# From tile 8 on, the attention products' feature blocks rotate over the four column places and are turned back by transfers

## The chip, the cores and the metric

One core of one Trainium2 chip. The metric is device time in microseconds (us) of one launch; 847.02 us is the median of three runs of the kernel before (846.87, 847.02, 848.01). PE is TensorE, PEld its weight loads, DVE VectorE, ACT ScalarE, POOL GpSimd, SP SyncE, whose queue issues nearly all transfers (DMAs).

## What is computed

Three stages one after the other: a linear recurrence over time with decay (the attention), a feed-forward layer with a maximum of three projections, and a gated layer with a norm.

```python
for t in range(S):                       # attention, B=4, H=8, S=768, D=48
    cur = u * k[t] outer v[t]
    y[:, :, t] = r[t] @ (state + cur)
    state = w * state + k[t] outer v[t]
x = y as 3072 tokens x 384 features      # H * D = 384
h = maximum(maximum(x @ w1, x @ w2), x @ w3)          # 384 -> 768
x = h @ w_out                                         # 768 -> 384
xn = x / sqrt(mean(x*x) + 1e-6) * rms_g
out = (silu(xn @ w_gate) * (xn @ w_val)) @ w_out2     # 384 -> 1536 -> 384
```

## The kernel before

Attention goes in 24 tiles of 128 time steps of one batch row: tile i belongs to chunk c = i // 4 (six chunks) and row b = i % 4. A stage u (0 to 5) is the first layer on the 512 tokens of chunk u: 18 slots `a_l1` (six blocks f times three projections w, nine matmuls of 512 columns each) and six slots `a_out`. The tiles of chunk u + 1 and later are woven between the slots of stage u: tiles 8 to 11 in stage 1, and so on, up to tiles 20 to 23 in stage 4; stage 5 has none. After each slot the loop of the schedule runs the steps that are due, so the order on every engine is the order in which this Python code calls them. A step list gives three steps for each tile: `block(i)`, `ahead(i + 2)` and `ahead_b(i + 2)`. After each step one queued load of a later tile is issued on SP. `tick` (weight conversion) runs after some slots and puts a load, three ACT steps, one or five DVE steps and stores into the queues.

`block(i)` is: score products of the next tile (`pe_a`, tile `pa`) and their masking on DVE (`mix`, L302, into `Dg`), the outputs of tile i (`pe_y`, L352, PSUM tile `py`), their split (`fin`), and the key-value product (`pe_st`, L321, PSUM tile `pkv`), which ACT masks (L308, tile `kv`) and POOL adds to the state `T` (L327, L329). `py` has 128 partitions by 3 x 128 columns. The 384 features are 12 blocks of 32; four column places (lanes) n of PE, 32 columns each, write the partitions 32n to 32n + 31 of the three k. Place n below 3 holds offset 32n of head pair k, place 3 holds head pair 3. A block at offset 0 or 64 lies in one head and needs one product `Dg`, one at offset 32 lies in two heads and needs two; from chunk 1 on each needs one more with the state. So the places have 6, 9, 6 and 7 products, 28 in all. They are issued round by round, one product of each place that still has any. Each product of f32 numbers is two matmul instructions (passes) in the profile.

`fin` splits `py` into a high and a low part: ACT copies it to `xt[u][:, 0]` (L365), DVE writes the difference to `xt[u][:, 1]` (L366). `xt[u]` is the moving operand of the first layer (L73 to L75, PSUM tile `pl`). A `pl` bank (four in all) is freed by ACT (L412, w = 0) or DVE (L415, w = 1, 2). Four slots later PE takes it again.

Of the kernel before, what the change touches and what calls it, by code (L numbers as in the profile page):

```python
# [10 lines left out]
F32R = mybir.dt.float32r  # L11
# [5 lines left out]
ALU = mybir.AluOpType  # L17
# [14 lines left out]
HF = 2  # L32
U0T = (1, 1, 1, 1, 0, 1, 1, 1, 0, 1, 1, 1, 1, 1, 1, 0, 1, 1, 1, 0, 1, 1, 1, 1, 1, 1, 1, 1, 1, 1)
LEAD = 4
DM, FF1, FF2 = 384, 768, 1536
NB = S // 128
NT = B * NB
# [4 lines left out]
def r32(ap):  # L42
    return ap.bitcast(F32)
# [3 lines left out]
def rwkv_moe_kernel(ctx, tc, rkT, rkv, wd, ub, cst, rg, w1p, wo1p, w2p, out):  # L47
    nc = tc.nc
    act, dve, pool, pe, sync = nc.scalar, nc.vector, nc.gpsimd, nc.tensor, nc.sync
# [8 lines left out]
    tp = sT.enter_context(tc.tile_pool(name="att", bufs=1, side="right"))  # L58
# [127 lines left out]
    def load_next(n=1):  # L186
        for _ in range(n):
            if loads:
                loads.pop(0)()

    def load_tile(i):
        if i >= NT:
            return
        a = tp.tile([128, 2, NP, 128], F32, tag="raw", bufs=3, name=f"raw{i}")
        t = tp.tile([128, VO + NP * 144], F32, tag="tm", bufs=3, name=f"tm{i}")
        raw_t[i], tm_t[i] = a, t
        loads.append(lambda: sync.dma_start(a[0:64], rows64[96 * i:96 * i + 64]))
        if i < NT - 1:
            loads.append(lambda: sync.dma_start(a[64:128], rows64[96 * i + 48:96 * i + 112]))
        else:  # L200
            loads.append(lambda: (sync.dma_start(a[64:112], rows64[96 * i + 48:96 * i + 96]),
                                  sync.dma_start(a[112:128], rows64[96 * i:96 * i + 16])))
        loads.append(lambda: sync.dma_start(t[:, 0:VO], rkv[i, :, 0:VO]))
        loads.append(lambda: sync.dma_start(t[:, VO:], rkv[i, :, VO:]))
# [47 lines left out]
    def prep_raw(i):  # L252
        raw = raw_t.pop(i)
        st[i] = dict(raw=raw, tm=tm_t.pop(i))
        if i == 0:
            dve.tensor_tensor(out=raw[:, 1], in0=raw[:, 1], in1=qk[:, 1], op=ALU.mult)
            dve.tensor_tensor(out=raw[:, 0], in0=raw[:, 0], in1=qk[:, 0], op=ALU.mult)
        else:
            dve.tensor_tensor(out=raw, in0=raw, in1=qk, op=ALU.mult)

    def prep(i):
        prep_raw(i)
        s = st[i]
        tm = s["tm"]
        ru = tp.tile([128, DM], F32, tag="ru", name=f"ru{i}")
        eng = dve if i < NRU else pool
        eng.tensor_tensor(out=ru, in0=tm[:, 0:DM], in1=usb, op=ALU.mult)
        eng.tensor_tensor(out=ru, in0=ru, in1=tm[:, DM:2 * DM], op=ALU.mult)
        s["ru"] = ru

    def prep_b(i):
        s = st[i]
        a8 = tp.tile([128, H], F32, tag="a8", bufs=2, name=f"a8{i}")
        ru = s["ru"]
        dve.tensor_reduce(out=a8, in_=ru.rearrange("p (h d) -> p h d", d=D), op=ALU.add,  # L275
                          axis=mybir.AxisListType.X)
        Dg = tp.tile([128, H, 128], F32, tag="Dg", bufs=2, name=f"Dg{i}")
        pool.affine_select(out=Dg, in_=a8.unsqueeze(2).to_broadcast([128, H, 128]),  # L278
                           pattern=[[0, H], [1, 128]], channel_multiplier=-1, base=0,
                           compare_op=ALU.is_equal, fill=0.0)  # L280
        s["Dg"] = Dg

    def prep2(i):
        if i // B < NB - 1:
            k = st[i]["tm"][:, DM:2 * DM]
            pool.tensor_tensor(out=k, in0=k, in1=kt, op=ALU.mult)

    def pe_a(i):
        s = st[i]
        raw = s["raw"]  # L290
        pa = [psx.tile([128, NP, 128], F32, tag="x", name=f"pa{i}_{j}") for j in range(2)]
        for pr in range(NP):
            for j in range(2):
                sl = slice(64 * j, 64 * j + 48)
                pe.matmul(pa[j][:, pr], raw[sl, 1, pr], raw[sl, 0, pr], start=True, stop=True)  # L295
        s["pa"] = pa

    def mix(i):
        s = st[i]
        dg = s["Dg"].rearrange("p (r j) t -> p r j t", j=2)  # L300
        for j in range(2):
            dve.copy_predicated(out=dg[:, :, j], mask=cmask.unsqueeze(1).to_broadcast([128, NP, 128]),  # L302
                                data=s["pa"][j])
# [6 lines left out]
    def pe_st(i):  # L310
        s = st[i]
        c, b = divmod(i, B)
        if c == NB - 1:
            return
        tm = s["tm"]
        v3 = tm[:, VO:].rearrange("p (r q e) -> p r q e", q=3, e=D)
        pk = psx.tile([128, NP, D], F32, tag="x", name=f"pkv{i}")
        for pr in range(NP):
            for j in range(2):
                o = DM + 96 * pr + 48 * j  # L320
                pe.matmul(pk[64 * j:64 * j + 64, pr], tm[:, o:o + 64], v3[:, pr, 2 * j], start=True, stop=True)  # L321
        if c == 0:
            mask_kv(Tst[b], pk)
        else:
            kv = tp.tile([128, NP, 96], F32, tag="kv", name=f"kv{i}")
            mask_kv(kv, pk)
            pool.tensor_tensor(out=Tst[b], in0=Tst[b],  # L327
                               in1=w128.unsqueeze(2).to_broadcast([128, NP, 96]), op=ALU.mult)
            pool.tensor_tensor(out=Tst[b], in0=Tst[b], in1=kv, op=ALU.add)  # L329

    def pe_y(i):
        s = st[i]
        c, b = divmod(i, B)
        tm = s["tm"]
        py = s["py"] = psx.tile([128, 3, 128], F32, tag="x", name=f"py{i}")
        lanes = []
        for n in range(4):
            lane = []
            for k in range(3):
                pr, o = (k, 32 * n) if n < 3 else (3, 32 * k)  # L340
                ops = [(tm[:, VO + 144 * pr + 48 * j + o:VO + 144 * pr + 48 * j + o + 32],
                        s["Dg"][:, 2 * pr + j]) for j in range(2) if o != (64, 0)[j]]
                if c > 0:
                    ops.append((Tst[b][:, pr, o:o + 32], s["raw"][:, 0, pr]))
                for m, (l, r) in enumerate(ops):
                    lane.append((py[32 * n:32 * n + 32, k], l, r, m == 0, m == len(ops) - 1))
            lanes.append(lane)
        for m in range(max(map(len, lanes))):
            for lane in lanes:
                if m < len(lane):  # L350
                    o, l, r, start, stop = lane[m]
                    pe.matmul(o, l, r, start=start, stop=stop)  # L352

    xt = {}

    def fin(i):
        s = st[i]
        u, m = divmod(i, B)
        if m == 0:
            xt[u] = ap_.tile([128, 2, 3, 512], F32R, tag="x", bufs=2, name=f"x{u}")  # L360
        xh, xl = xt[u][:, 0], xt[u][:, 1]
        o = 128 * m
        cs = slice(o, o + 128)
        y = s["py"]
        act.copy(xh[:, :, cs], y)  # L365
        dve.tensor_tensor(out=xl[:, :, cs], in0=y, in1=r32(xh[:, :, cs]), op=ALU.subtract)  # L366

    def att_steps():
        def block(i):
            if i + 1 < NT:  # L370
                pe_a(i + 1)
                mix(i + 1)
            pe_y(i)
            fin(i)
            pe_st(i)
            load_tile(i + 3)

        def ahead(i):
            load_next(2)
            prep(i)  # L380

        def ahead_b(i):
            load_next(1)
            prep_b(i)
            prep2(i)

        for i in range(NT):
            yield lambda i=i: block(i)
            yield lambda i=i: ahead(i + 2) if i + 2 < NT else None
            yield lambda i=i: ahead_b(i + 2) if i + 2 < NT else None  # L390

    hs, sB = {}, {}
# [98 lines left out]
    with tc.manual_schedule():  # L491
# [14 lines left out]
        for _ in range(WARM):  # L506
            pe.matmul(pw[:, 0:128], r32(ones), r32(ones), start=True, stop=True)
        steps = list(att_steps())
        pos = 0
        tick(TKI[0])  # L510
# [113 lines left out]
        def split(h, lo, x, lo_eng):  # L624
            act.copy(h, x)
            lo_eng.tensor_tensor(out=lo, in0=x, in1=r32(h), op=ALU.subtract)
# [29 lines left out]
        for u in range(NB):  # L656
# [13 lines left out]
            for n, sl in enumerate(slots):  # L670
# [5 lines left out]
                if u:  # L676
                    want = -(-len(todo) * (n + 1) // (len(slots) - LEAD))
                elif n < 3 * HF:
                    want = min(4, n + 1)
                else:  # L680
                    want = 4 + -(-(len(todo) - 4) * (n + 1 - 3 * HF) // (len(slots) - LEAD - 3 * HF))
                want = min(len(todo), want)
# [393 lines left out]
```

## Time and profile before

| what | before |
|---|---|
| median of three runs | 847.02 us |
| profiled execution | 845.96 us |
| its span, first to last instruction | 844.3 us |
| mean granted clock of PE | 0.987 of full |
| PE busy | 824.3 us, 98% |
| DVE busy | 461.2 us, 55% |
| ACT busy | 413.7 us, 49% |
| matmul instructions on L352 | 1248 (768 with `Dg`, 480 with the state), 17 to 351 us |

The profile is of one execution. Busy time says how much of the span an engine worked; the chain of waits follows the work that ended last back to what released it. Times in rows count from the first instruction. The profiled execution and the median differ by 1.06 us.

### The profile page before, as it was taken

To read this page: it belongs to the slowest core of one execution; us is meant where nothing else is said; L and a number is where in the kernel's file an instruction comes from. 1 tells how busy PE (TensorE), PEld (TensorE's weight loads), DVE (VectorE), ACT (ScalarE), POOL (GpSimd) and SP (SyncE) were. 2 spreads that over 40 slices of the span, in tenths; PEclk is the share of its full clock that TensorE was granted. 3 is DMA by queue.
4 is the path that set the end of the run, shared out by engine and by line. 5 is a ranking of instruction groups with operands and counts; after the bars stand their busy time and mean duration, and the time that the engine had idled before them with its cause. 6 is when DMAs were issued, how large, how long until landed. Compare 5 with 4: busy or idle time off the path is not lost.

```text
span 844.3 us, 13450 instructions
## 1 busy us (share of the span) xinstructions
PE 824.3 (98%) x5206; PEld 682.8 (81%) x5206; DVE 461.2 (55%) x706; ACT 413.7 (49%) x762; POOL 231.9 (27%) x201
## 2 busy tenths in 40 slices
PE   7889999999999999999999999999999999999996
PEld 6778888888888888888788888887888888888885
DVE  6888968748747646327346433823554463333342
ACT  1898865454544451124466554645444444444441
POOL 2388836544444422015354440001000000000000
PEclk8799999999999999999999999999999999999998
DMA  8997777664754641052576630624331064333011
GB/s 243 269 268 211 242 238 217 204 192 139 226 166 157 208 145 48 2 198 108 207 284 218 228 153 0 262 105 175 125 130 52 25 237 144 119 112 113 1 38 41
DMA packets 48915, 131.87 MB, mean 156 GB/s; under 512 B 6982, under 2 KB 19782, under 8 KB 44236
## 3 DMA queue, kind: packets, MB, share of 16 engines
q1 hardware_dynamic: 46972, 116.59, 42.7%
q0 software_dynamic: 1728, 14.16, 4.4%
q8 instruction: 43, 0.70, 0.4%
q14 instruction: 28, 0.23, 0.1%
q10 hardware_dynamic: 144, 0.20, 0.1%
HBM read 97.08 MB, written 33.84 MB: 155 GB/s over the span
## 4 chain that ended last, share of the span: by engine, by line
PE 93%; DMA 2%; DVE 2%; ACT 1%; issue 1%; POOL 0%; SPq 0%; DVEq 0%; POOLq 0%; ACTq 0%
PE pl L73 9%; PE pl L74 9%; PE pl L75 8%; PE po L75 6%; PE po L73 6%; PE po L74 6%; PE py L352 5%; PE px L73 4%; PE px L75 4%; PE px L74 4%; PE pb L73 3%; PE pc L73 3%; PE pb L75 3%; PE pb L74 3%; PE pa L73 3%; PE pa L75 3%
## 5 line engine op out<-in xcount | busy, mean ns | idle before, releaser
L73 PE MATMUL pl<-x,w_a 128*128 128x512 f32 (+1 forms) x342 | 132.0, 386 | 2.3 <-ACT x L365 2.3
L74 PE MATMUL pl<-x,w_a 128*128 128x512 f32 (+1 forms) x342 | 129.8, 380 | 0.7 <-DVE x L366 0.7
L75 PE MATMUL pl<-x,w_a 128*128 128x512 f32 (+1 forms) x342 | 129.4, 378 | 0.0
L851 DVE TENSOR_TENSOR v<-pb,es 128x512 f32<-128x512 f32 x36 | 24.9, 692 | 176.1 <-PE pb L75 176.1
L415 DVE TENSOR_TENSOR c<-pl,c 128x512 f32<-128x512 f32 (+1 forms) x76 | 50.1, 659 | 54.9 <-PE pl L75 53.6
L73 PEld LDWEIGHTS pl<-x,w_a 128*128 128x128 f32 x342 | 64.5, 189 | 15.9 <-ACT x L365 2.6
L74 PEld LDWEIGHTS pl<-x,w_a 128*128 128x128 f32 x342 | 64.6, 189 | 12.4 <-DVE x L366 1.1
L75 PEld LDWEIGHTS pl<-x,w_a 128*128 128x128 f32 x342 | 64.5, 188 | 12.2
L760 ACT CAST hb<-si 128x512 fp32r<-128x512 f32 x36 | 22.4, 622 | 81.7 <-DVE si L854 81.7
L417 ACT CAST h1h<-c 128x512 fp32r<-128x512 f32 (+1 forms) x32 | 19.0, 593 | 77.5 <-DVE c L415 77.5
L119 DVE SCALAR_TENSOR_TENSOR wf<-wf,wraw 128x384 uint32<-128x384 uint32 x60 | 49.5, 828 | 7.9 <-ACT wraw L112 6.8
L278 POOL TENSOR_SCALAR_AFFINE_SELECT Dg<-a 128x1024 f32<-128x1024 f32 x24 | 30.0, 1248 | 77.7 <-DVE a L275 60.3
L552 POOL TENSOR_TENSOR ws<-gv,ws 128x576 fp32r<-128x576 f32 x24 | 36.0, 1502 | 53.6 <-ACT ws L551 53.6
L302 DVE COPY_PREDICATED Dg<-csb,pa 128x512 f32<-128x512 uint32 x48 | 32.8, 738 | 31.5 <-PE pa L295 27.1
L352 PE MATMUL py<-Dg,tm 128*32 128x128 f32 x768 | 48.3, 292 | 0.0
L352 PEld LDWEIGHTS py<-Dg,tm 128*32 128x32 f32 x768 | 40.6, 116 | 4.0 <-issue 0.6
L73 PE MATMUL pb<-f,ws 128*128 128x512 f32 x108 | 42.5, 393 | 0.7 <-ACT pb L829 0.6
L73 PE MATMUL pc<-z,ws 128*128 128x512 f32 x108 | 42.1, 390 | 0.3 <-ACT pd L846 0.3
L73 PE MATMUL pa<-f,ws 128*128 128x512 f32 x108 | 42.1, 389 | 0.0
L74 PE MATMUL px<-hb,wo 128*128 128x512 f32 x108 | 42.0, 389 | 0.0
L75 PE MATMUL pb<-f,ws 128*128 128x512 f32 x108 | 42.0, 389 | 0.0
L75 PE MATMUL pa<-f,ws 128*128 128x512 f32 x108 | 42.0, 389 | 0.0
(180 smaller groups left out, 2065.9 us busy)
## 6 DMA issues: line engine op xcount, KB each, us to landing
ws<-w2s SPq DMA_DIRECT2D x24, 1152.0 KB, 5.4
wraw<-in_w2p SPq DMA_DIRECT2D x36, 384.0 KB, 5.1
w2s<-ws POOLq DMA_DIRECT2D x12, 1152.0 KB, 5.9
raw<-in_rkT SPq DMA_DIRECT2D x47, 256.0 KB, 4.0
tm<-in_rkv SPq DMA_DIRECT2D x24, 384.0 KB, 5.3
tm<-in_rkv SPq DMA_DIRECT2D x24, 288.0 KB, 5.4
wraw<-in_w1p SPq DMA_DIRECT2D x18, 384.0 KB, 8.9
w2d<-wf SPq DMA_DIRECT2D x36, 192.0 KB, 4.0
```

What stands on the lines that cost most here:

```text
L73: pe.matmul(o, lh, rh, start=start, stop=False, **kw)
L74: pe.matmul(o, lh, rl, start=False, stop=False, **kw)
L75: pe.matmul(o, ll, rh, start=False, stop=stop, **kw)
L119: dve.scalar_tensor_tensor(out=wu, in0=wu, scalar=3, in1=cbits(n).bitcast(U32), op0=ALU.logical_shift_left, op1=ALU.bitwise_or)
L278: pool.affine_select(out=Dg, in_=a8.unsqueeze(2).to_broadcast([128, H, 128]), pattern=[[0, H], [1, 128]], channel_multiplier=-1, base=0, c ...
L302: dve.copy_predicated(out=dg[:, :, j], mask=cmask.unsqueeze(1).to_broadcast([128, NP, 128]), data=s["pa"][j])
L352: pe.matmul(o, l, r, start=start, stop=stop)
L415: dve.tensor_tensor(out=c1[:, :n], in0=p[:, :n], in1=c1[:, :n], op=ALU.max)
L417: act.copy(hh, c1[:, :n])
L552: lo_eng.tensor_tensor(out=t[:, 1, sl], in0=r[:, sl], in1=r32(t[:, 0, sl]), op=ALU.subtract)
L760: act.copy(hh, x)
L851: dve.tensor_tensor(out=v1, in0=Bk, in1=es, op=ALU.add)
```

## The change

For tiles from 8 on the block of head pair k moves on by `TURN[k]` places: k = 0 by one, k = 1 not at all, k = 2 by three. All four places then have seven products. The result of k = 0 and k = 2 stands in the wrong partitions; it is split into a new tile `yt` (128 partitions by 2 k by high and low by 128), and two transfers for each k write it to the right partitions of `xt[u]`. Only k = 1 is split into `xt[u]` directly. The transfers are issued on SP at the beginning of the step `ahead`, which now exists for the last two tiles too.

```diff
+TURN = (1, 0, 3)
+TURNED = 8
...
-                pr, o = (k, 32 * n) if n < 3 else (3, 32 * k)
+                m = (n + TURN[k] * (i >= TURNED)) % 4
+                pr, o = (k, 32 * m) if m < 3 else (3, 32 * k)
...
-        act.copy(xh[:, :, cs], y)
-        dve.tensor_tensor(out=xl[:, :, cs], in0=y, in1=r32(xh[:, :, cs]), op=ALU.subtract)
+
+        def split(hi, lo, y):
+            act.copy(hi, y)
+            dve.tensor_tensor(out=lo, in0=y, in1=r32(hi), op=ALU.subtract)
+
+        if i < TURNED:
+            split(xh[:, :, cs], xl[:, :, cs], y)
+            return
+        t = tp.tile([128, 2, 2, 128], F32R, tag="yt", name=f"yt{i}")
+        split(t[:, 0], t[:, 1], y[:, 0::2])
+        split(xh[:, 1, cs], xl[:, 1, cs], y[:, 1])
+
+        def turn():
+            for n, k in enumerate((0, 2)):
+                o = 32 * TURN[k]
+                sync.dma_start(r32(xt[u][o:128, :, k, cs]), r32(t[0:128 - o, :, n]))
+                sync.dma_start(r32(xt[u][0:o, :, k, cs]), r32(t[128 - o:128, :, n]))
+
+        turns.append(turn)
...
         def ahead(i):
-            load_next(2)
-            prep(i)
+            while turns:
+                turns.pop(0)()
+            if i < NT:
+                load_next(2)
+                prep(i)
```

Three places in the order of the instructions; line numbers of the changed kernel are higher. First PE, the outputs of tile 8, the last eleven rows of products and the key-value product behind them (x4: four products in a row). Before:

```order
L352 MATMUL py_1420<-raw_896,T_94 32x128
L352 MATMUL py_1420<-Dg_1111,tm_897 32x128 x2
L352 MATMUL py_1420<-raw_896,T_94 32x128
L352 MATMUL py_1420<-Dg_1111,tm_897 32x128
L352 MATMUL py_1420<-raw_896,T_94 32x128
L352 MATMUL py_1420<-Dg_1111,tm_897 32x128 x4
L352 MATMUL py_1420<-raw_896,T_94 32x128 x4
L352 MATMUL py_1420<-Dg_1111,tm_897 32x128 x2
L352 MATMUL py_1420<-raw_896,T_94 32x128
L352 MATMUL py_1420<-Dg_1111,tm_897 32x128
L352 MATMUL py_1420<-raw_896,T_94 32x128
L321 MATMUL pkv_1452<-tm_897 64x48 x8
```

And all 28 products of the same tile with the change:

```order
L355 MATMUL py_1420<-Dg_1111,tm_897 32x128 x5
L355 MATMUL py_1420<-raw_896,T_94 32x128 x4
L355 MATMUL py_1420<-Dg_1111,tm_897 32x128 x5
L355 MATMUL py_1420<-raw_896,T_94 32x128
L355 MATMUL py_1420<-Dg_1111,tm_897 32x128
L355 MATMUL py_1420<-raw_896,T_94 32x128 x2
L355 MATMUL py_1420<-Dg_1111,tm_897 32x128
L355 MATMUL py_1420<-raw_896,T_94 32x128
L355 MATMUL py_1420<-Dg_1111,tm_897 32x128 x4
L355 MATMUL py_1420<-raw_896,T_94 32x128 x4
L323 MATMUL pkv_1455<-tm_897 64x48 x8
```

Before, the last two products are both of place 1; now the last four are of four places.

Second DVE, from the mask of tile 9 to the maximum of the second slot of stage 1 (`c<-pl`), before:

```order
L302 COPY_PREDICATED Dg_1267<-csb,pa_0_1408 128x4x128
L302 COPY_PREDICATED Dg_1267<-csb,pa_1_1409 128x4x128
L366 TENSOR_TENSOR x_1449<-py_1420,x_1449 128x3x128
L119 SCALAR_TENSOR_TENSOR wf_1382<-wf_1382,wraw_1334 128x384
L415 TENSOR_TENSOR c_0_0_1406<-pl_0_1_0_1477,c_0_0_1406 128x512
```

With the change, the semaphores that an instruction waits for at its end:

```order
L304 COPY_PREDICATED Dg_1267<-csb,pa_0_1408 128x4x128 [waits PE_49,Pool_49]
L304 COPY_PREDICATED Dg_1267<-csb,pa_1_1409 128x4x128 [waits PE_49]
L371 TENSOR_TENSOR yt_1450<-py_1420,yt_1450 128x256 [waits Activation_49]
L371 TENSOR_TENSOR x_1449<-py_1420,x_1449 128x128 [waits Activation_49]
L121 SCALAR_TENSOR_TENSOR wf_1382<-wf_1382,wraw_1334 128x384 [waits DMAHW6_49,DMAHW1_49]
L440 TENSOR_TENSOR c_0_0_1406<-pl_0_1_0_1480,c_0_0_1406 128x512 [waits DMAHW0_49,PE_49,Pool_49]
```

One subtraction has become two, each behind a copy of ACT. Beside it ACT, the copies of the same tile, before:

```order
L412 COPY c_0_0_1406<-pl_0_0_0_1396 128x512
L365 CAST x_1449<-py_1420 128x3x128
L308 ACTIVATE kv_1461<-pkv_1452,csb 128x4x48
L308 ACTIVATE kv_1461<-pkv_1452,m_86 128x4x48
L109 ACTIVATE wf_1471<-wraw_1357 128x384
```

With the change:

```order
L437 COPY c_0_0_1406<-pl_0_0_0_1396 128x512 [waits PE_49,Pool_49]
L370 CAST yt_1450<-py_1420 128x256 [waits PE_49]
L370 CAST x_1449<-py_1420 128x128 [waits DVE_49]
L310 ACTIVATE kv_1464<-pkv_1455,csb 128x4x48 [waits PE_49]
L310 ACTIVATE kv_1464<-pkv_1455,m_86 128x4x48
L111 ACTIVATE wf_1474<-wraw_1357 128x384 [waits DMAHW7_49,DMAHW4_49,DMAHW3_49]
```

Between the copies, which read one PSUM tile, stands a wait for DVE's first subtraction.

Third SP, around the loads of tile 11 (`raw`, `tm`), behind tile 8, before:

```order
L197 DMA raw_1466<-in_rkT 64x1024
L98 DMA wraw_1469<-in_w2p 128x384
L147 DMA w2d<-wf_1359 128x384
L199 DMA raw_1466<-in_rkT 64x1024
L203 DMA tm_1467<-in_rkv 128x768
L204 DMA tm_1467<-in_rkv 128x576
```

With the change:

```order
L199 DMA raw_1469<-in_rkT 64x1024
L100 DMA wraw_1472<-in_w2p 128x384
L149 DMA w2d<-wf_1359 128x384
L383 DMA x_1449<-yt_1450 96x2x128
L384 DMA x_1449<-yt_1450 32x2x128
L383 DMA x_1449<-yt_1450 32x2x128
L384 DMA x_1449<-yt_1450 96x2x128
L201 DMA raw_1469<-in_rkT 64x1024
L205 DMA tm_1470<-in_rkv 128x768
L206 DMA tm_1470<-in_rkv 128x576
```

The four transfers stand between the two halves of a load.

## Rows read from the trace of the kernel before

**Rows 1.** The page: busy time of PE; granted clock in 40 slices, in tenths.

```profile
PE 824.3 (98%) x5206; PEld 682.8 (81%) x5206; DVE 461.2 (55%) x706; ACT 413.7 (49%) x762; POOL 231.9 (27%) x201
PEclk8799999999999999999999999999999999999998
```

**Rows 2.** Busy time of each engine (x instructions), granted clock, DMA share, GB/s, one stretch.

```profile
109.00:352.00 243.00, 243.00 (x2136) 200.74 (x2135) 156.68 (x256) 110.13 (x208) 99.97 (x84) 1.00 0.53 166
```

**Rows 3.** Chain that ended last, outputs of tile 11: start us, us, what.

```profile
155.48 2.09 PE py L352 x56
```

**Rows 4.** Timeline of PE, tile 11: start us, us, engine, line, operation, count.

```profile
155.41 0.43 PE L352 MATMUL py<-Dg,tm 128*32 128x128 f32 x8
...
156.97 0.38 PE L352 MATMUL py<-Dg,tm 128*32 128x128 f32 x2
157.19 0.38 PE L352 MATMUL py<-raw,T 128*32 128x128 f32 x2
157.50 0.67 PE L321 MATMUL pkv<-tm 128*64 128x48 f32 x16
```

**Rows 5.** Tile `py`: duration ns min/median/max, first and last start us, forms.

```profile
L352 PEld LDWEIGHTS py<-raw,T x480: 110/110/110, 54.0 to 350.7; 128*32 128x32 f32 x160
...
L365 ACT CAST x<-py x24: 466/479/490, 20.1 to 351.1; 128x384 fp32r<-128x384 f32 x24
L366 DVE TENSOR_TENSOR x<-py,x x24: 530/558/559, 20.6 to 351.6; 128x384 fp32r<-128x384 f32 x24
```

**Rows 6.** Timeline of PE, tile 3 (first chunk, no state products).

```profile
41.73 1.50 PE L352 MATMUL py<-Dg,tm 128*32 128x128 f32 x32
43.17 0.67 PE L321 MATMUL pkv<-tm 128*64 128x48 f32 x16
```

**Rows 7.** Line 412 of ACT: duration ns min (128x256), median, max (128x512).

```profile
L412 ACT COPY c<-pl x38: 364/586/593, 37.0 to 400.8; 128x512 f32<-128x512 f32 x34, 128x256 f32<-128x256 f32 x4
```

**Rows 8.** Timeline of DVE, then of POOL, around tile 8.

```profile
107.01 0.29 DVE L133 TENSOR_TENSOR wf<-wf,wf 128x128 f32<-128x128 f32 x1
...
116.89 0.95 DVE L133 TENSOR_TENSOR wf<-wf,wf 128x128 f32<-128x128 f32 x1 [2.51 <-DMA w2d<-wf]
...
118.91 1.05 DVE L133 TENSOR_TENSOR wf<-wf,wf 128x128 f32<-128x128 f32 x1
119.88 1.35 DVE L302 COPY_PREDICATED Dg<-csb,pa 128x512 f32<-128x512 uint32 x2
121.14 0.53 DVE L366 TENSOR_TENSOR x<-py,x 128x384 fp32r<-128x384 f32 x1
...
122.06 0.68 DVE L415 TENSOR_TENSOR c<-pl,c 128x512 f32<-128x512 f32 x1
...
116.67 1.02 POOL L329 TENSOR_TENSOR T<-T,kv 128x384 f32<-128x384 f32 x1 [1.61 <-ACT kv L308]
...
118.80 1.01 POOL L268 TENSOR_TENSOR ru<-ru,tm 128x384 f32<-128x384 f32 x1
```

**Rows 9.** Timeline of PE: sixth slot of stage 1, which takes the second slot's bank.

```profile
122.86 0.44 PE L73 MATMUL pl<-x,w_a 128*128 128x512 f32 x1
```

**Rows 10.** Timeline of DVE and of PE: a bank freed, and taken again.

```profile
212.49 0.68 DVE L415 TENSOR_TENSOR c<-pl,c 128x512 f32<-128x512 f32 x1
...
217.60 0.39 PE L73 MATMUL pl<-x,w_a 128*128 128x512 f32 x1
```

**Rows 11.** Timeline of SP's queue after tile 11: start us, us of the issue.

```profile
158.12 0.59 SPq L199 DMA_DIRECT2D raw<-in_rkT  x1
```

**Rows 12.** Timeline of PE: first product of stage 2.

```profile
174.55 0.39 PE L73 MATMUL pl<-x,w_a 128*128 128x512 f32 x1
```

**Rows 13.** DMA issues: count, KB each, median us from issue to landing.

```profile
x2d<-x2s SPq DMA_DIRECT2D x18, 256.0 KB, 2.1
...
wraw<-in_w1p SPq DMA_DIRECT2D x18, 384.0 KB, 8.9
```

**Rows 14.** Wait instructions on PE's queue ahead of `py`: ns min/median/max.

```profile
L352 PEldq EVENT_SEMAPHORE  x25: 51/51/51, 15.4 to 344.7; - x25
```

More of the change, by code (lines that the diff above doesn't have):

```diff
@@ L364, in fin @@
         y = s["py"]
-        act.copy(xh[:, :, cs], y)
-        dve.tensor_tensor(out=xl[:, :, cs], in0=y, in1=r32(xh[:, :, cs]), op=ALU.subtract)
+        def split(hi, lo, y):
[13 more added lines that the diff above has]
+        turns.append(turn)
+    turns = []
     def att_steps():
@@ L388, in att_steps @@
             yield lambda i=i: block(i)
-            yield lambda i=i: ahead(i + 2) if i + 2 < NT else None
+            yield lambda i=i: ahead(i + 2)
             yield lambda i=i: ahead_b(i + 2) if i + 2 < NT else None
```

## The prediction

> **What bounds the kernel now.** I read the busy time first: TensorE (PE) is busy for 98% of the span, and its granted clock is full in nearly every slice [rows 1]. The change touches tiles 8 to 23, which run between 109 and 352 us, so I asked for that stretch alone: PE is busy in 243.00 of 243.00 us at a granted clock of 1.00, against 157 us for VectorE (DVE) and 110 us for ScalarE (ACT); the DMA engines are 53% busy [rows 2]. There no other engine's work shows as a PE gap, so what PE does less is time won, as long as nothing new makes it wait.
>
> What does PE spend on the attention product `py`? The chain of waits gives 2.09 us for the 56 matmul instructions of one tile [rows 3]: 28 products, each two PE passes. Products go round the four lanes (the 32-column places). Place 1 holds three blocks at offset 32, which need three products each; so one lane has nine products, the others six, six and seven. The instruction rows of a tile show what this costs. A lane starts a pass when its weight load is done, and this load takes 110 ns [rows 5]. At the start all four lanes run together (eight instructions from 155.41 us); at the end the long lane runs alone: two passes from 156.97, two from 157.19, and the next group at 157.50 [rows 4]. So a pass costs about 0.109 us whether one lane or four use it, and the tile lasts as long as its longest lane: 18 passes. A tile of the first chunk has no state products; its longest lane has 12 passes, and it takes 43.17 - 41.73 = 1.44 us [rows 6]. (2.09 - 1.44) / 6 = 0.108 us a pass, the same figure from two lengths.
>
> **The products.** The rotation gives every lane seven products. The count stays 28, the longest lane falls from 18 passes to 14. Each tile from 8 on saves 4 x 0.108 = 0.43 us, and 16 tiles save **6.9 us**. The new tail has four lanes that end together, staggered by up to 0.02 us (by the four-lane starts of the first rows), where one lane ended before: 16 x 0.02 = 0.3 us given back. The row of the 12-pass tile has unequal lanes too, so the 14-pass tile lies between two measured shapes; I see no reason for a gain beyond 7.0.
>
> **The split.** ACT's copy of 128x384 (479 ns) and DVE's subtraction (558 ns) [rows 5] become two each: 128x256 and 128x128. The second ACT copy waits for the first DVE subtraction, since both read the same PSUM tile; so the four go in turn. Nearest rows: an ACT copy of 128x256 takes 364 ns [rows 7], a DVE subtraction of 128x128 takes 0.29 us [rows 8]. The four make about 0.36 + 0.40 + 0.3 + 0.29 = 1.35 us, against 1.04. ACT and DVE are each held up by some 0.5 us more per tile, as each stands in its queue while the other works. Queued behind on ACT are the two masked copies of the key-value product and a weight conversion, on DVE a conversion and the maximum that frees a PSUM bank for PE. Over the stretch DVE has 86 us and ACT 133 us idle, and 16 x 0.5 = 8 us fits in it. This costs nothing wherever the bank is freed in good time, and from the trace one place is tight.
>
> That place is tile 8. DVE comes late from the weight work: the mask (119.88), the split (121.14), the maximum (122.06 to 122.74) [rows 8]; PE takes this bank again at 122.86 [rows 9]. The slack is 0.12 us, and PE will arrive 0.43 earlier. If DVE begins the mask at the same time and the split is 0.5 longer, PE waits 0.5 + 0.43 - 0.12 = **0.8 us** there. Against it: the last three of DVE's subtractions before the mask (0.95 us the first, 1.05 the last, against 0.29 for one of the same form at 107.01) run beside POOL's additions and products [rows 8]. The first of these, at 116.67, waits for ACT's masked copy, and ACT will now stand in its split until DVE has passed the mask. So POOL falls quiet while DVE runs, DVE's three shrink by 3 x 0.7 = 2.1 us, more than the 0.8. I take 0 and keep 0.8 as the other end. The Trainium skill, page "SBUF — State Buffer", section "SBUF: two separate sides", says that VectorE with two SBUF inputs and GpSimd hold one shared port pair by turns, each for a whole instruction; the stretched rows agree, and by that rule the wait is 0. For the 70 slots after it, up to 352 us, I took the same difference, bank freed to bank used: the smallest is 217.60 - (212.49 + 0.68) = 4.4 us [rows 10], so half a microsecond is covered.
>
> **The transfers.** Each tile adds four DMAs (96 or 32 partitions, 512-byte pieces, 256 KB a tile in sum) on SP's queue, ahead of the second half of the load of tile i+3. They wait for the second subtraction. Behind them SP holds three loads of a later tile, a weight load and a weight store. Four issues cost about 4 x 0.5 = 2 us of SP (0.59 for one of the loads [rows 11]); the loads are wanted a tile later, 243 / 16 = 15 us on, so this is covered. Who waits for the transfers? The first product of the next stage. For tile 11, `py` ends at 157.50 [rows 4] and that product starts at 174.55 [rows 12]: 17 us. The split takes 1.4, the issues 2, the landing between 2.1 us (256 KB out of SBUF) and 8.9 us (the slowest kind of load) [rows 13]: 5.5 to 12.3, so **nothing** on the path. If a landing exceeded 13.6 us, the excess would be paid four times, once a stage. That product and the seventh of its slot wait for up to six semaphores each, where one wait instruction takes PE's queue 51 ns [rows 14]: at most 2 x 5 x 0.051 = 0.5 us a stage, 2 us in all, and 0 where PE still has matmuls queued. Each tile's `py` carries such an instruction today while PE is busy without a gap [rows 2], so I take 0.
>
> **Sum.** -6.9 + 0.3 + 0 + 0 = -6.6 us. The profiled execution took 845.96 us with a span of 844.3; it should become 839.4 with a span of 837.7. It lies 1.06 below the median of 847.02, so I put the forecast at 847.0 - 6.6 = **840.4 us**.
>
> **Rivals.**
> (1) The lanes balance, but the longer split chain, or PE's added semaphore waits, or DVE waiting for a weight store that SP now issues later, holds a PSUM bank: 0.8 us at tile 8 and as much in two or three more places, some 2 us: 842.4, within 841.4 to 844.5. For it: 0.12 us of slack at tile 8. Against: the idle time of DVE and ACT, and over 4 us of slack elsewhere. The Trainium skill, page "TensorEngine Tiling (Array Packing)", section "Performance Considerations", warns that tiling speeds up TensorE but not the emptying of PSUM, which may become the bottleneck; by that rule this rival would hold throughout. The row of the whole stretch, with DVE busy for 157 of 243 us, speaks against it.
> (2) Slower: the turned blocks land late. Each of the four next stages would begin with a wait. To lose 0.2% they must eat 6.6 + 1.7 = 8.3 us, 2.1 us a stage, so a landing would have to take 13.6 + 2.1 = 15.7 us from the last issue. With 18 us: 4 x 4.4 = 17.6, 847.0 + 11.0 = 858. Against: 8.9 us is the longest median among the kinds of transfer [rows 13].
> (3) No change: PE is limited by the number of instructions, not by the longest lane. 56 stay 56 and the time stays 847.0. Against: 56 instructions in 2.09 us are 0.037 each, while in the lone tail one takes 0.109. Or something with a fixed pace (SP, the weight conversion) takes over; then 846 to 847.
>
> **How the numbers follow.** Forecast (839.6 to 841.4): 0.72. Rival 1: 0.17. Rival 2: 0.04. Rival 3: 0.05. Below 839.6: 0.02. The range takes in the forecast and the larger part of rival 1: 839.5 to 843.0. A measurement of this kernel can tell about 0.2%, 1.7 us. Faster by more than that: forecast, the part below it and nearly all of rival 1, 0.91; within: 0.05; slower: 0.04.
>
> **What would show it.** Right: `py` of tiles 8 to 23 at 1.65 to 1.68 us, `py` of tiles 0 to 7 unchanged, no PE wait on a DMA at the four stage starts, PE busy time some 7 us lower. Rival 1 shows as PE idle on ACT or DVE (at the sixth slot after 108 us first of all), rival 2 as PE idle on the transfers from the `yt` tile, rival 3 as `py` still at 2.09. The forecast is wrong if PE's stretch from tile 8 to tile 23 is not 6 to 7 us shorter.

## The result, and the profile after

The changed kernel takes 838.7 us (median of seven runs, 836.05 to 841.52) beside 846.98 us for the kernel before (seven runs, 843.45 to 852.26): a ratio of 0.9907, 95% interval 0.9882 to 0.9931 (the ratios in this document are those on record; they differ a little from the quotients of the medians, here 0.9902). The forecast was 840.4 us in a range of 839.5 to 843.0. The sign and the mechanism came as argued; the time lies 0.8 us below the range. The lines of the code that the rows name have moved: `pe_y` is L355, the split L370 and L371, the transfers L383 and L384, the first layer L75 to L77, the maximum L440.

The page first, beside [rows 1]: PE's busy time fell from 824.3 to 814.1 us, and its share of the span stayed at 98%.

```profile
PE 814.1 (98%) x5206; PEld 673.2 (81%) x5206; DVE 464.7 (56%) x722; ACT 415.3 (50%) x778; POOL 234.4 (28%) x201
PEclk8999999999999999999999999999999999999999
```

Second, the stretch of tiles 8 to 23 alone, as in [rows 2] (busy time of each engine, granted clock, DMA share, GB/s). PE is busy in all of it, and the DMA engines work for 61% of it where it was 53%:

```profile
109.60:343.00 233.40, 233.40 (x2113) 191.86 (x2112) 158.72 (x270) 108.65 (x218) 100.73 (x83) 1.00 0.61 187
```

Third, the outputs of tile 11 in the chain of waits, and PE's timeline under it, which answer [rows 3] and [rows 4]:

```profile
151.95 1.67 PE py L355 x56
153.62 0.60 PE pkv L323 x16
...
153.00 0.40 PE L355 MATMUL py<-Dg,tm 128*32 128x128 f32 x8
153.22 0.40 PE L355 MATMUL py<-raw,T 128*32 128x128 f32 x8
153.55 0.67 PE L323 MATMUL pkv<-tm 128*64 128x48 f32 x16
```

The 56 instructions take 1.67 us instead of 2.09. At the end eight instructions start together at 153.00 and eight at 153.22: four lanes of two passes each. The lane that ran alone is gone. The sixteen tiles from 8 on take 1.66 or 1.67 us each, tiles 4 to 7 still 2.09.

Fourth, the rows of the two tiles that the split and the transfers use (duration ns min/median/max; for the transfers the issue, then KB and median us to landing from the list of DMA issues):

```profile
L370 ACT CAST x<-py x24: 266/267/487, 19.8 to 343.1; 128x128 fp32r<-128x128 f32 x16, 128x384 fp32r<-128x384 f32 x8
L371 DVE TENSOR_TENSOR x<-py,x x24: 291/292/558, 20.3 to 343.4; 128x128 fp32r<-128x128 f32 x16, 128x384 fp32r<-128x384 f32 x8
L370 ACT CAST yt<-py x16: 362/373/373, 113.3 to 342.2; 128x256 fp32r<-128x256 f32 x16
L371 DVE TENSOR_TENSOR yt<-py,yt x16: 399/425/425, 116.9 to 342.6; 128x256 fp32r<-128x256 f32 x16
...
L383 SPq DMA_DIRECT2D x<-yt x32: 604/625/1635, 118.4 to 344.4; - x32
...
DMA to landing us min/median/max: 1.9/2.2/4.9
...
x<-yt SPq DMA_DIRECT2D x32, 96.0 KB, 2.6
...
x<-yt SPq DMA_DIRECT2D x32, 32.0 KB, 2.0
```

The four steps of the split make 0.373 + 0.425 + 0.267 + 0.292 = 1.36 us, as estimated (1.35). The trace tells the landing of 23 of the 64 transfers; the slowest of these took 4.9 us. After tile 11 SP begins to issue at 155.54, just behind the end of DVE's first subtraction (155.51), and the four issues take 3.70 us, one of them 1.64; the last begins at 158.63:

```profile
155.54 0.66 SPq L383 DMA_DIRECT2D x<-yt  x1
156.25 0.65 SPq L384 DMA_DIRECT2D x<-yt  x1
156.95 1.64 SPq L383 DMA_DIRECT2D x<-yt  x1
158.63 0.61 SPq L384 DMA_DIRECT2D x<-yt  x1
...
170.62 0.39 PE L75 MATMUL pl<-x,w_a 128*128 128x512 f32 x1
```

Stage 2 begins at 170.62. Even with the longest landing that is known, this tile's last block would be there at 163.5, 7 us early. In the list of PE's waits over the whole execution nothing waits on a transfer from `yt`. The two largest rows of that list, and two that name ACT and DVE in the first layer (line, what ended it, us, times, longest):

```profile
PE pa L297 <- issue: 3.3, 2, 1.7
PE pk L238 <- DVE Rtab L231: 2.1, 1, 2.1
...
PE pl L75 <- ACT x L370: 1.1, 2, 0.9
...
PE pl L76 <- DVE x L371: 0.7, 2, 0.5
```

All of these lie in the first 51 us, ahead of the first changed instruction.

**Where the 9.9 us of the profiled executions come from.** Three marks on PE divide the two spans: the first product of stage 1, the first product of stage 5, the last product.

| stretch, us | before | after | difference |
|---|---|---|---|
| start to stage 1 (tiles 0 to 7, stage 0; not changed) | 108.65 | 106.41 | -2.24 |
| stage 1 to stage 5 (tiles 8 to 23) | 258.78 | 252.07 | -6.71 |
| stage 5 to the last product | 469.22 | 469.18 | -0.04 |
| last product to the end of the span | 7.60 | 6.62 | -0.98 |
| span | 844.25 | 834.28 | -9.97 |

The stretch that the change touches gives 6.71 us, 16 x 0.42, against 6.6 in the sum. The other 3.2 us come from a beginning and an end that the change leaves as they are. So the question for the experiments: does the change shorten these too, or do they vary by themselves?

**Tile 8**, the one place where a wait of 0.8 us was at stake [rows 8, 9]. DVE, then ACT, POOL and PE in the kernel after:

```profile
114.84 0.29 DVE L135 TENSOR_TENSOR wf<-wf,wf 128x128 f32<-128x128 f32 x1 [2.61 <-DMA w2d<-wf]
115.17 0.29 DVE L135 TENSOR_TENSOR wf<-wf 128x128 f32<-128x128 f32 x1
115.49 0.29 DVE L135 TENSOR_TENSOR wf<-wf,wf 128x128 f32<-128x128 f32 x1
115.70 1.35 DVE L304 COPY_PREDICATED Dg<-csb,pa 128x512 f32<-128x512 uint32 x2
116.94 0.42 DVE L371 TENSOR_TENSOR yt<-py,yt 128x256 fp32r<-128x256 f32 x1
117.69 0.29 DVE L371 TENSOR_TENSOR x<-py,x 128x128 fp32r<-128x128 f32 x1 [0.33 <-ACT x L370]
...
118.36 0.68 DVE L440 TENSOR_TENSOR c<-pl,c 128x512 f32<-128x512 f32 x1
...
117.39 0.27 ACT L370 CAST x<-py 128x128 fp32r<-128x128 f32 x1 [3.75 <-DVE yt L371]
...
118.43 1.02 POOL L331 TENSOR_TENSOR T<-T,kv 128x384 f32<-128x384 f32 x1 [5.51 <-ACT kv L310]
...
120.20 0.39 PE L75 MATMUL pl<-x,w_a 128*128 128x512 f32 x1
```

ACT stands in its split until DVE has passed the mask (3.75 us), so its masked copy comes later, and POOL, which needs that copy, stands idle until 118.43. DVE's three subtractions now take 0.29 us each, where the first and the last took 0.95 and 1.05. The maximum ends at 119.04, and PE takes the bank at 120.20: the distance grew from 0.12 to 1.16 us. (The 0.12 was no slack: PE's weight load in front of that product stood 0.20 us for DVE's maximum in the kernel before.) The split is enough for this, without the rotation too: in all seven profiles that have it at tile 8 (the change three times, experiments 2, 4, 8 and 9) the three subtractions take 0.29 us each; in the three of before they take 0.73 to 1.06. It isn't needed for it: in experiment 7, without the split, POOL came late as well, and they take 0.29. The Trainium skill, page "SBUF — State Buffer", section "SBUF: two separate sides", has VectorE with two SBUF inputs and GpSimd hold a shared port pair by turns; this trace agrees: 0.29 us with POOL quiet, 0.95 to 1.05 beside its additions.

### The profile page after: what moved, and what is told of

Same layout as the page of the kernel before. It is cut to its first block, busy times and chain, and to the rows that moved or that the text cites. A ratio compares the mean times of both kernels' runs of the same rounds, so it can differ in the third digit from the quotient of the medians.

```text
span 834.3 us, 13625 instructions
## 1 busy us (share of the span) xinstructions
PE 814.1 (98%) x5206; PEld 673.2 (81%) x5206; DVE 464.7 (56%) x722; ACT 415.3 (50%) x778; POOL 234.4 (28%) x201
## 4 chain that ended last, share of the span: by engine, by line
PE 93%; DMA 3%; DVE 2%; ACT 1%; issue 1%; POOL 0%; SPq 0%; DVEq 0%; POOLq 0%; ACTq 0%
PE pl L75 9%; PE pl L76 9%; PE pl L77 9%; PE po L75 6%; PE po L77 6%; PE po L76 6%; PE py L355 4%; PE px L75 4%; PE px L76 4%; PE px L77 4%; PE pb L75 3%; PE pc L75 3%; PE pb L77 3%; PE pb L76 3%; PE pa L75 3%; PE pa L76 3%
## 5 line engine op out<-in xcount | busy, mean ns | idle before, releaser
L75 PE MATMUL pl<-x,w_a 128*128 128x512 f32 (+1 forms) x342 | 131.7, 385 | 1.1 <-ACT x L370 1.1
L77 PE MATMUL pl<-x,w_a 128*128 128x512 f32 (+1 forms) x342 | 129.6, 379 | 0.7 <-POOL w_a L130 0.7
L75 PEld LDWEIGHTS pl<-x,w_a 128*128 128x128 f32 x342 | 64.3, 188 | 14.3 <-ACT x L370 1.4
L77 PEld LDWEIGHTS pl<-x,w_a 128*128 128x128 f32 x342 | 64.3, 188 | 13.3 <-POOL w_a L130 0.9
L440 DVE TENSOR_TENSOR c<-pl,c 128x512 f32<-128x512 f32 (+1 forms) x76 | 50.1, 659 | 44.4 <-PE pl L77 42.6
L75 PE MATMUL pb<-f,ws 128*128 128x512 f32 x108 | 42.5, 393 | 0.7 <-ACT pb L854 0.6
L75 PE MATMUL pc<-z,ws 128*128 128x512 f32 x108 | 42.1, 390 | 0.3 <-ACT pd L871 0.3
L75 PE MATMUL pa<-f,ws 128*128 128x512 f32 x108 | 42.0, 389 | 0.0
L77 PE MATMUL pb<-f,ws 128*128 128x512 f32 x108 | 42.0, 389 | 0.0
L76 PE MATMUL pc<-z,ws 128*128 128x512 f32 x108 | 42.0, 389 | 0.0
L77 PE MATMUL pa<-f,ws 128*128 128x512 f32 x108 | 42.0, 389 | 0.0
L76 PE MATMUL pa<-f,ws 128*128 128x512 f32 x108 | 42.0, 389 | 0.0
L76 PE MATMUL pb<-f,ws 128*128 128x512 f32 x108 | 42.0, 389 | 0.0
```

Of the source, the lines that this page charges most:

```text
L75: pe.matmul(o, lh, rh, start=start, stop=False, **kw)
L76: pe.matmul(o, lh, rl, start=False, stop=False, **kw)
L77: pe.matmul(o, ll, rh, start=False, stop=stop, **kw)
L440: dve.tensor_tensor(out=c1[:, :n], in0=p[:, :n], in1=c1[:, :n], op=ALU.max)
```

## The experiments

Experiments 1 to 4, 5 to 8 and 9 to 11 each ran together on one chip and share its runs of the kernel before. "Beside" gives the median of those. Two theories on the 3.2 us: **A**, the beginning and the end vary from execution to execution, and the change is worth what its own stretch shows; **B** or **C**, the change (or how it is compared) gives something more, systematically.

**1. One tile only.**

```diff
-TURNED = 8
+TURNED = 23
```

> Only tile 23 is turned; the program up to 340 us does the same work as before, but the yt tile has its place in SBUF. Theory A (the change is worth 0.42 us a tile and the rest of the measured gain is chance of the granted clock in the first 40 us): 0.4 us below the kernel before, ratio 0.9995, inside the noise. Theory B (the new layout of the program or of SBUF makes the first 40 us shorter, by about 1.6 us in the median): some 2.0 us below, ratio 0.9976.

Measured: 844.46 us (842.89 to 852.81, 12 runs) beside 847.8 (28 runs), ratio 0.9973, 0.9944 to 1.0002. In the chain of waits of this kernel the last two tiles' outputs read

```profile
335.54 2.09 PE py L355 x56
...
348.09 1.67 PE py L355 x56
```

From the outputs of tile 23 to stage 5 PE needs 18.13 us, before 18.55: one turned tile is worth one tile, 0.42 us. (Stage 1 to stage 5 takes 258.48 us, 0.30 less than before; the other 0.1 goes at tile 8, which is not turned here.) The median fell by 3.3 us, and the ratio is theory B's 0.9976 almost to the digit. By themselves this ratio and that of experiment 2 (0.9976 too) would speak for B; experiment 5 takes that from them, since it gives a lower one for the unchanged program of before.

**2. The split and the transfers without the rotation.** Every place keeps its block, and the transfers copy to the same partitions.

```diff
-                m = (n + TURN[k] * (i >= TURNED)) % 4
+                m = n
...
-                sync.dma_start(r32(xt[u][o:128, :, k, cs]), r32(t[0:128 - o, :, n]))
-                sync.dma_start(r32(xt[u][0:o, :, k, cs]), r32(t[128 - o:128, :, n]))
+                sync.dma_start(r32(xt[u][0:128 - o, :, k, cs]), r32(t[0:128 - o, :, n]))
+                sync.dma_start(r32(xt[u][128 - o:128, :, k, cs]), r32(t[128 - o:128, :, n]))
```

> From tile 8 on the split in two and the four transfers are kept, but no block is rotated and the transfers write to the same partitions. All costs of the change without its gain. Theory A: py stays at 2.09 us, PE does not wait, 0 to 0.8 us above the kernel before, ratio 1.000 to 1.001. Theory B: some 1.6 us below, ratio 0.998. Rival 1 of the prediction (the split chain holds PSUM banks): 1 to 4 us above, seen as PE idle on ACT or DVE after 108 us.

Measured: 847.1 us (12 runs) beside 847.8, ratio 0.9976, 0.9954 to 0.9998. Stage 1 to stage 5: 258.71 us, against 258.78 before (the 0.07 is the wait at tile 8 that is gone). So what the change adds costs 0 on the path, within 0.1 us, as the sum had it. The interval of the ratio lies just below 1, as does that of the unchanged copy of before in experiment 5.

**3. The rotation without the way back.** The condition of the old split is always taken; this kernel leaves out `yt` and the transfers, so the features stand in wrong rows.

```diff
-        if i < TURNED:
+        if True:
```

> The blocks are rotated from tile 8 on, but the result is split as before and not turned back: yt and the 64 transfers are left out, so the features stand in wrong rows and the output is not the reference's. Theory A (transfers and split cost nothing on the path): py at 1.67 us, the same time as the change, 6.7 us below the kernel before, ratio 0.992. If the transfers or the split cost PE time, this is faster than the change by that time. Theory B, if the layout with yt brings 1.6 us: 6.7 below, and the change 8.3 below.

Measured: 840.55 us (837.42 to 842.52, 6 runs), ratio 0.9907, 0.9873 to 0.9942. Stage 1 to stage 5: 252.07 us, the same as with the change. Experiments 2 and 3 say the same from both sides: the whole gain of the stretch is the lanes' (258.71 - 252.07 = 6.64 us, 16 x 0.415), and the transfers are hidden.

**4. From tile 4 on.** Could the four tiles of stage 0 give 0.42 us each as well?

```diff
-TURNED = 8
+TURNED = 4
```

> The rotation begins with tile 4. Four more tiles at 0.42 us: theory A 20 x 0.42 = 8.4 us below the kernel before, ratio 0.990, if stage 0, where DVE and ACT are nearly full, covers the longer split. Theory B: 10 us below, ratio 0.988. If DVE or ACT bounds stage 0, the four tiles bring nothing there and cost up to 0.8 us each: 4 to 7 us below, with PE idle on ACT or DVE before 108 us.

Measured: 841.59 us (838.43 to 846.96, 11 runs), 6.2 below its own runs of before, a ratio of 0.9922, and 2.7 above the change's 838.9 (below). Its `py` of tiles 4, 5 and 7 takes 1.66 or 1.67 us, that of tile 6 takes 3.09. From the outputs of tile 4 to stage 1 it needs 56.93 us, where the change needs 54.79; with four tiles gained it should be 53.1. Here rival 1 came true. Its DVE, then its ACT, and PE, around tile 5:

```profile
71.20 1.38 DVE L304 COPY_PREDICATED Dg<-csb,pa 128x512 f32<-128x512 uint32 x2
73.72 0.42 DVE L371 TENSOR_TENSOR yt<-py,yt 128x256 fp32r<-128x256 f32 x1 [1.15 <-ACT yt L370]
...
76.24 1.43 DVE L261 TENSOR_TENSOR raw<-raw,qk 128x1024 f32<-128x1024 f32 x1
...
71.16 0.56 ACT L111 ACTIVATE wf<-wraw 128x384 f32<-128x384 f32 x1 [0.68 <-DMA wraw<-in_w1p]
...
73.33 0.36 ACT L370 CAST yt<-py 128x256 fp32r<-128x256 f32 x1
...
77.77 1.25 PE L297 MATMUL pa<-raw 48*128 48x128 f32 x16 [1.74 <-issue]
```

ACT waits for a weight load, then works off its conversion and comes to the split at 73.33. DVE stands 1.15 us for it, so the product that prepares `raw` for the next scores ends at 77.67 (76.24 + 1.43), and PE, idle for 1.74 us, begins the scores at 77.77. The profile puts that idle time down to "issue"; the end of DVE's row, 0.1 us ahead, names the releaser better. Then the granted clock falls (third column from the end; PE's busy time first):

```profile
54.40:78.00 23.60, 21.86 (x245) 18.47 (x246) 19.74 (x29) 18.68 (x41) 18.97 (x18) 1.00 0.64 183
78.00:79.50 1.50, 1.50 (x28) 1.38 (x31) 1.47 (x3) 1.44 (x4) 0.53 (x1) 0.86 0.81 194
79.50:83.00 3.50, 3.50 (x69) 3.06 (x60) 3.50 (x8) 3.00 (x7) 0.79 (x1) 0.57 1.02 355
83.00:111.33 28.33, 28.33 (x197) 23.04 (x198) 24.00 (x32) 24.02 (x49) 21.65 (x19) 1.00 0.82 256
```

At a mean of 0.57 (for the most part the lower of its two levels, 1.2 of 2.4 GHz) these 3.5 us did the work of 2.0. So 1.7 us of idle time and 1.7 us of clock (3.5 x 0.43 + 1.5 x 0.14) make up most of the missing 3.8.

A further loss lies behind stage 0, at the place that the prediction named: the sixth slot of stage 1, after tile 8. DVE begins its three subtractions 10.1 us into stage 1, where the change begins them at 8.4, so its maximum ends at 125.61, and PE waits (its weight load for 0.81 us):

```profile
124.93 0.68 DVE L440 TENSOR_TENSOR c<-pl,c 128x512 f32<-128x512 f32 x1
...
125.67 0.50 PE L75 MATMUL pl<-x,w_a 128*128 128x512 f32 x1 [0.39 <-DVE c L440]
```

Stage 1 to stage 5 takes 252.78 us here, 0.71 more than with the change. POOL was quiet and the three subtractions took 0.29 us each; that cover alone isn't enough where DVE begins them late. Together the profile puts this kernel 2.14 + 0.71 = 2.85 us behind the change, and the medians lie 2.7 apart. In stage 0 ACT and DVE are busy for 47 and 50 of 55 us, in the stretch of tiles 8 to 23 for 109 and 159 of 233: there the longer split has room, here it has none. The Trainium skill, page "TensorEngine Tiling (Array Packing)", section "Performance Considerations", warns that tiling doesn't speed up the emptying of PSUM, which may then become the bottleneck. From tile 8 on the change's own traces speak against it as a limit; in stage 0 the engines that empty PSUM do become one, though by their queues rather than by the split's own 1.36 us.

**5 and 6. The kernel before and the change once more**, unchanged, as if each were a variant.

> The kernel before, unchanged, timed as if it were a variant. Theory A (the 1.3 us by which the change came out lower than the 840.4 forecast are the beginning and the tail of the span, which vary from execution to execution): ratio 1.000 within 0.003, about 847.0 us, and the stretch from the start of stage 1 to the start of stage 5 is 258.8 us as in the kernel before, while the start of stage 1 lies anywhere from 106 to 112 us. Rival B (something in how two kernels are run beside each other favours the second): ratio about 0.998, 845.5 us.

> The change, once more. Theory A: the stretch from stage 1 to stage 5 is 252.1 us again (6.7 less than the kernel before), the median lies 6.7 us below the kernel before of the same call within 1.5 us, ratio 0.992. Rival C (the change also makes the beginning of the span shorter, though its instructions are the same there): 8 us or more below, ratio 0.990 again, and the start of stage 1 again near 106 us.

Measured: the copy of before 844.02 us (843.04 to 847.16, 8 runs) beside 846.48 (19 runs), a ratio of 0.9967, 0.9944 to 0.9989, for the same program. The copy of the change 838.6 us (836.32 to 842.52, 6 runs), ratio 0.9914, 0.989 to 0.9938. The difference of the two copies is 5.4 us, that of the change and the 19 runs of before 7.9. So the interval of this copy of before doesn't hold 1, for the same program; 0.3% is not yet a finding. Stage 1 to stage 5: 258.92 and 252.08 us, 6.84 apart.

**7 and 8. Is it the granted clock at the start?** In the profile of before PE's granted clock averages 0.78 from 12 to 50 us, where PE waits again and again. Both kernels with 24 products of constants into the warm-up's bank, so that PE is busier there:

```diff
+        def fill(n):
+            for _ in range(n):
+                pe.matmul(pw[:, 0:128], r32(ones), r32(ones), start=True, stop=True)
+
+        fill(WARM)
...
+        fill(10)
...
+        fill(6)
...
+            if pos == 0:
+                fill(8)
```

> The kernel before with 24 products of constants into the warm-up's bank added where TensorE waits at the beginning (10 after the first pe_a, 6 after the tables, 8 after the first step). Their results are not used. If the half-clock stretches of the first 50 us follow from TensorE's early waits, they should be fewer or shorter: start of stage 1 at 105 to 107 us, 2 to 4 us below the kernel before, ratio 0.996, and a smaller spread of the times. If not, the time is the kernel before's, or up to 2 us above it where the added products stand in the way (ratio 1.000 to 1.002).

> The change with the same 24 added products. The two are independent by Theory A: 6.7 us below the kernel before with the fill, whatever that gives: 836 to 838 us where the fill helps, ratio 0.988; 840 us where it does not, ratio 0.992. From stage 1 to stage 5: 252.1 us either way.

Measured: before with the fill 846.17 us (844.07 to 855.0, 12 runs), ratio 1.0008, 0.9983 to 1.0032; the change with it 840.41 (6 runs), ratio 0.9927, 0.991 to 0.9943, 5.8 us apart. Stage 1 to stage 5 takes 258.71 and 252.63 us. The second is 0.56 above the expected 252.1: at 229.23 us PE stands for DVE's subtraction `h1l` (its weight load for 0.54 us), in stage 2, where the change's own profiles lose at most 0.1. Whether the split brings that wait isn't shown. The stretch from 12 to 50 us, granted clock third from the end, DMA share and GB/s behind it: before, the change, before with the fill, the change with the fill, and the kernel of experiment 2:

```profile
12.00:50.00 38.00, 30.50 (x331) 26.22 (x332) 29.18 (x45) 25.73 (x54) 17.66 (x17) 0.78 1.05 281
...
12.00:50.00 38.00, 29.06 (x341) 25.06 (x341) 32.45 (x47) 27.87 (x58) 19.87 (x19) 0.87 1.04 281
...
12.00:50.00 38.00, 31.20 (x378) 27.84 (x377) 29.20 (x47) 26.73 (x56) 18.09 (x18) 0.91 1.04 288
...
12.00:50.00 38.00, 32.46 (x390) 29.04 (x390) 32.90 (x48) 29.23 (x61) 21.02 (x20) 0.91 1.04 300
...
12.00:50.00 38.00, 29.07 (x311) 24.60 (x312) 26.21 (x40) 22.75 (x47) 15.07 (x15) 0.73 1.04 266
```

The fill did what it was for: the clock of the stretch rises to 0.91. The time didn't follow: stage 1 starts at 107.91 us in before with the fill, at 108.65 without, and the medians are the same. So the 2 to 4 us that were hoped for from the clock don't come; less than 1.5 us isn't excluded by the interval. What all these rows share is a full DMA share, 1.04 to 1.05. Their rate differs, from 266 to 300 GB/s, and the start of stage 1 goes with it: 112.40 us at 266, 105.33 at 300; over the twelve profiles that load the same there (all but experiment 4) the correlation is -0.86. But the granted clock of the stretch goes with the start too: -0.77, and in the ten profiles without the fill -0.85, as much as the rate's. Only the fill parts the two, for it moved the clock and not the median. That the pace of the loads sets the beginning is thus a guess that fits, and isn't shown: a beginning that gets on faster also asks for its loads sooner.

**9. A longest lane of eight products.** The one number of the sum that matters most, the pass, tried at a third length.

```diff
-TURN = (1, 0, 3)
+TURN = (1, 0, 2)
```

> The change with another turn of the third feature block (by two places, not three): the lanes have 7, 7, 6 and 8 products, so the longest has 16 passes, between the kernel before (18) and the change (14). Theory A (a tile's time is the longest lane's passes at 0.109 us): py of tiles 8 to 23 takes 1.88 us, stage 1 to stage 5 takes 258.8 - 16 x 0.21 = 255.4 us, some 3.4 below the kernel before. Rival D (what counts is that no lane runs alone, by how many lanes share the end): 1.67 us again, 252.1. Rival E (only four lanes that are alike run at full speed): nearer to 2.09.

Measured: 840.94 us (838.8 to 846.43, 12 runs) beside 845.52 (23 runs), ratio 0.9949, 0.9928 to 0.9971. Tile 11 in its chain of waits:

```profile
153.88 1.88 PE py L355 x56
```

Stage 1 to stage 5: 255.38 us, 3.40 below before, as expected to 0.1 us. Lanes of 7, 7, 6 and 8 products take neither 1.67 nor 2.09: the longest one counts, 0.21 us a product of two passes, whatever the other three do. (16 passes at 0.109 us are 1.74; the rest is the end of the tile, below.)

**10 and 11. Both kernels a third time.**

> The kernel before, built and loaded once more. If the whole of the difference between one build of it and the next is chance, its median lies between 844 and 848 us with the stretch from stage 1 to stage 5 at 258.8 to 259.0 us, and the start of stage 1 at 106 to 112 us.

> The change, built and loaded once more. Theory A: 6.7 us below the mean of the kernel before over its builds (some 846.5), so 838 to 841.5 us; stage 1 to stage 5 at 252.1 us; start of stage 1 at 106 to 112 us as in the kernel before. Rival C (the beginning is really shorter in the change): stage 1 starts at 106 to 107 us a fourth time, while the kernel before of this call starts it above 108.

Measured: before 845.15 us (12 runs), ratio 0.9996, 0.9975 to 1.0016; the change 838.98 (836.55 to 840.6, 6 runs), ratio 0.9914, 0.9885 to 0.9943. Between the two medians lie 6.2 us. And the beginnings have changed places: stage 1 starts at 106.62 us in before, at 108.15 in the change. So theory C, a beginning of 106 to 107 us each time with the change, falls.

| profiled execution | start to stage 1 | stage 1 to last product | last product to end |
|---|---|---|---|
| before | 108.65 | 728.00 | 7.60 |
| before, second | 109.04 | 728.12 | 7.90 |
| before, third | 106.62 | 728.18 | 7.43 |
| change | 106.41 | 721.25 | 6.62 |
| change, second | 107.09 | 721.23 | 7.46 |
| change, third | 108.15 | 721.33 | 7.89 |

The middle column is the same to 0.2 us within each kernel, and 6.8 us apart between them. The other two vary by up to 2.4 and 1.3 us within one kernel. All runs together, the median of before is 846.4 us (97 runs), that of the change 838.9 (19 runs): 7.5 apart. The spreads (2.35 and 1.85 us) give this difference an interval of about 1 us either way if each run counted by itself, and experiment 5 says that they count for less. With each set of runs counted once, the six of before average 846.0 us and the three of the change 838.8, 7.2 apart. Whether the 0.4 to 0.7 us above 6.8 are more than chance stays open. No version tried beats the change.

## Why the prediction was right, and where it failed

**The products.** Right, in both terms: 18 passes to 14, 0.42 us a tile, 6.71 us in all. In PE's rows of tile 11 the passes of one place start 0.109 us apart, before, after and in experiment 9, so four passes fewer are 0.436 us; and the four places of the changed tile end 0.02 us apart, which gives back the 0.3 us of the sum. 16 x 0.416 makes 6.66, experiments 2 and 3 differ by 6.64, and the rest is the 0.07 us of waiting that went at tile 8. A tile is not its passes alone (18 x 0.109 = 1.96, not 2.09): from the start of its last pass to the next group PE takes 0.20 us, in the kernel before (157.29 to 157.50) as after (153.35 to 153.55), and this drops out of the difference. PE's busy time fell by 10.2 us, not by some 7: 6.7 of it lie in the stretch of the change, the rest in the beginning.

**The split.** Right, in size and in cost: 1.36 us a tile, nothing on the path, by experiments 2 and 3. At tile 8 the cover was the one named, a quiet POOL; DVE's three subtractions shrank by 2.1 us, as forecast.

**The transfers.** Right: 2.0 and 2.6 us to land, no known landing above 4.9 (5.3 in the third profile of the change), no wait. SP's part was longer than thought (its four issues for tile 11 take from 155.54 to 159.24, where 2 us were put), and the 17 us still held it. They don't wait for the second subtraction: the first issue begins while it is still to come (155.85).

**The rivals.** 2 and 3 didn't happen. Rival 1 didn't happen in the three profiles of the change. It did in experiment 4, in a stage where ACT and DVE have no room and then, for 0.7 us, at tile 8 itself, so the 0.8 us kept as the other end was a fair price; and the wait of 0.56 us in experiment 8 is of its kind.

**The step that failed** is the last one, from the sum to the range: the parts of the span that the change leaves as they are, the first 106 to 109 us and the last 7 to 8, were put at no difference, without a reason. In the two profiled executions they gave 2.24 + 0.98 = 3.2 us, half as much as the change itself; over three profiles of each kernel they vary by up to 2.4 and 1.3 us within one kernel. The sum was set on the median of three runs, 847.02, that lay within 1.2 us of each other, the low end was put 0.9 us below the forecast, with a chance of 0.02 for anything under 839.6, and a measurement was said to tell 0.2%. Three runs of one build can't show what six sets of runs of the same kernel did: medians from 844.0 to 847.8 us, single runs from 843.0 to 852.3, and two sets on one chip 0.3% apart.

With 2 us either way for these parts, from 838.4, the range would have held the result. The median of before was not what was off (846.98 with seven runs): the change came out 8.3 us below it, 6.7 to 6.9 of it in the stretch that was forecast. For the other 1.4 to 1.6 us of this measurement no cause is shown; chance between sets is enough for it, and a small further gain by the change isn't excluded. The profile of before gave a hint that was read for another purpose: the granted clock of its first slices isn't full [rows 1], so the beginning is no steady stretch.

## What to carry to other kernels

Where products share PE by column places, count the passes of the longest place, not the products: the tile's time followed it at three lengths, and a rotation that evens the places can be paid with transfers as long as they land well before the stage that reads them. Here a pass of that place took 0.109 us. Such a rearrangement lengthens the split on ACT and DVE, so look stage by stage at their idle time before spreading it. Compare kernels by a stretch of the trace between two products, which repeated to 0.2 us here, and give a forecast of the whole time the spread of the parts that the change doesn't touch.

## What was not expected of the hardware

A longer chain on ACT and DVE made DVE's work ahead of it shorter: with POOL kept idle for 5.51 us, three subtractions fell from about 1 us to 0.29 each. Part of that comes back behind the chain, where POOL now works: DVE's product for `raw` after the maximum takes 1.57 us at tile 8, where it took 1.21. And filling PE's early gaps raised its granted clock from 0.78 to 0.91 over 38 us and won no time, with the DMA engines' share at 1.04 all along.
